# W's third block with its mirrors in one gather, half columns of group two compared on GpSimd, two raw places left early

## The chip, the cores and the metric

The kernel runs on one core of a Trainium2 chip. The metric is the device time of one execution in microseconds (us), the median of three runs. The core's engines are TensorE (PE, matrix products), VectorE (DVE), ScalarE (ACT), GpSimd (POOL) and SyncE (SP). Here SyncE only issues DMA transfers; GpSimd issues gathers (indirect DMAs, which take a row index for each partition) and computes a little.

## The reference

One layer of an FNet block with a routed feed-forward network (FFN), for x of 2048 rows (tokens) by 576 columns, all in float32:

```
a = einsum("bsd,ed->bse", ln(x), dft_hid_re)
b = einsum("bsd,ed->bse", ln(x), dft_hid_im)
h = x + einsum("ts,bse->bte", dft_seq_re, a) - einsum("ts,bse->bte", dft_seq_im, b)
v = ln(h)
r = v @ w_r                               # one score per token
i = argmax(r)                             # capacity 1
y = (silu(v[i] @ w_gate) * (v[i] @ w_up)) @ w_down * sigmoid(r[i])
out = h + v;  out[i] += y
```

The DFT matrices are inputs: 2048 x 2048 and 576 x 576, real and imaginary parts. w_gate and w_up are 576 x 4608, w_down is 4608 x 576; all three are read whole, 31.9 MB.

## The kernel before

**Symmetry, used and tested.** A DFT matrix repeats itself in mirrors: row D - d is row d with the sign of the imaginary part changed, and so are the columns. The kernel computes with a half of each matrix only, and tests on the device, at every run, that the other half is what it should be: it loads the mirrors too, VectorE subtracts (or adds) a block and its mirror into a half of the scratch buffer Q, and ScalarE squares what is left and sums it into a column of DS (`add_square`, L368). If the sum isn't zero, a general path behind a branch at L1358 runs instead.

**The sequence matrix** (dram `ct`) comes in column blocks j = 0 to 15 with a real and an imaginary part i; blocks 1 to 5 form group one, blocks 6, 7, 0 and 8 group two (GROUPS). `c_first` loads a block that is computed with into a place of buffer D (SyncE, L357, 576 KB). `c_check(j, i)` loads its mirrors into raw places, by a gather on GpSimd (L301) and for a pair also by L357 and another gather, and compares: `off_s` (L375) twice and `off_t` (L380). `c_half` compares the halves of a block's own columns with each other: `off_h` (L387), 64 columns of each of 9 row tiles against the other 64. The raw places are the 7 parts of buffer R and those places of D that are free; the function `ring` (L804) hands out the first free one.

**The hidden matrix W** (dram `wt`, 576 rows of 1152: real and imaginary) is loaded by `load_w` in blocks A (rows 0 to 127), B (128 to 255) and C (rows 256 to 288, and the imaginary parts of 256 to 287 once more in partitions 64 to 95); `off_w` (L422 to L427) compares each with its mirror rows, gathered by index column `iw`, and its columns among themselves.

**Computing.** `seq` (L565) multiplies ct's blocks with the normalized, folded x (buffer XF); `keep` (L583) moves the sums into Z; `hid` (L610) multiplies with W; `residual` (L619, VectorE, one operand in PSUM as the name py says) adds x; ScalarE squares for the norm (L630), `dot_h` (L623) forms the scores, `scores` (L635) ends them, and ScalarE and GpSimd write h + v (L661, L654), stored by GpSimd's queue (L676, L678).

**FFN.** The weights come in 27 loads of 1152 KB on SyncE (L1200, and L1208 in two parts) into 17 spots, which are parts of R, D, XF, W, Z and Q that nothing needs any more. For the token VectorE and GpSimd multiply (L1217, L1224; L1228, 14 operations on GpSimd), ScalarE sums (L1233), the gate follows (L1244 to L1247), then TensorE's w_down (L1255) and the last row (L1268, L1278).

**The order.** No order is written by hand: every step is entered in a list (class `Plan`) with its engine, an estimated duration and what it needs, and the list is scheduled. Each engine then runs its instructions in that order, and SyncE and GpSimd each issue their transfers in theirs. An edit of a duration or a need moves steps elsewhere. `turn(n)` is a gather of n rows into a spare tile ahead of a store on GpSimd's queue.

The lines that tie a comparison to its buffers:

```
def ring(eng, f, mb, *args):
    u = free.pop(0)
    ring_last, d = load(eng, then(f, u, *args), mb, users[u], ring_last, LAST[eng])
...
    c_first(1, 1)
    for i in range(2):
        for j in GROUPS[1]:
            c_check(j, i)
    for c, m in HALVES[1]:
        c_half(1, c, m)
```

Of the kernel before, what the change touches and what calls it, by code (L numbers as in the profile page):

```python
# [142 lines left out]
def kernel(  # L143
# [237 lines left out]

    def off_h(g, c, n, i, u):

        o = Q[:, u % 2, i * 9 * n * HM : (i + 1) * 9 * n * HM].rearrange("p (c k m) -> p c k m", k=9, m=HM)
        t = DT[g, i][:, c : c + n]
        for k, op in enumerate((OP.subtract, OP.add)):
            dve.tensor_tensor(o[:, :, k::2, :], t[:, :, k::2, 0:HM], t[:, :, k::2, HM:P], op=op)  # L387

# [8 lines left out]
    def load_w(b, n):  # L397

        name = "ABC"[n % 3]
        if n < 3:  # L400
            t = W[name][:, :, 0:D]
            rows = wt[n * P : n * P + (P if n < 2 else 33), :].rearrange("p (c e) -> p c e", c=2)
            sp.dma_start(t if n < 2 else t[0:33], rows)
            if n == 2:
                sp.dma_start(W[name][64:96, 0, 0:D], wt[2 * P : HD, D : 2 * D])
# [7 lines left out]
    def wrap_w(n):  # L413

        act.activation(W[n][:, :, D : D + 1], W[n][:, :, 0:1], AF.Copy)

    def off_w(n, u):

        ps = W_ROWS[n]
        t, o = WM["ABC"[n]][0:ps], Q[0:ps, u % 2]  # L420
        re, im = W["ABC"[n]][0:ps, 0, :], W["ABC"[n]][0:ps, 1, :]
        dve.tensor_tensor(o[:, 0:D], t[:, 0:D], re[:, 0:D], op=OP.subtract)  # L422
        dve.tensor_tensor(o[:, D : 2 * D], t[:, D : 2 * D], im[:, 0:D], op=OP.add)
        o = o[:, 2 * D : 3 * D]
        dve.tensor_tensor(o[:, 0:287], re[:, 1:HD], re[:, D - 1 : HD : -1], op=OP.subtract)
        dve.tensor_tensor(o[:, 287:575], im[:, 1 : HD + 1], im[:, D - 1 : HD - 1 : -1], op=OP.add)
        dve.tensor_copy(o[:, 575:576], im[:, 0:1])  # L427

    W_ROWS = (P, P, 33)

# [75 lines left out]
    def biases(n0, n1):  # L506

        m, h = n1 - n0, (n1 - n0) // 2
        mean, rs, b = MX[:, n0:n1], RX[:, n0:n1], BX[:, n0:n1]
        pool.tensor_scalar(mean, XT[:, n0:n1], -1.0 / D, None, op0=OP.mult)  # L510
        pool.tensor_tensor(run_of(V0, n0, n1), run_of(MX, n0, n1), x_cols(n0, n1, 0), op=OP.add)
        pool.tensor_scalar(mean, mean, 2.0, None, op0=OP.mult)
        pool.tensor_tensor(b, mean, rs, op=OP.mult)
        q = FOLDED.index(ORDER[n0])
        d0 = XF[:, q : q + (h if n0 < 14 else 2), E0]
# [23 lines left out]
    def folded(k, part):  # L539
# [332 lines left out]

    WS, WL, WRAP = [], [], []

    def w_first():
        for n in range(3):
            LAST["SP"], d = load(
                "SP", then(load_w, None, n), (0.59, 0.59, 0.22)[n], LAST["SP"], users["W" + "ABC"[n]]
            )
            WL.append(d)  # L880

    def w_check():
        for n in range(3):
            u, d = ring("POOL", load_w, (0.59, 0.59, 0.16)[n], n + 3)
# [92 lines left out]
    for c, m in HALVES[0]:  # L977
        c_half(0, c, m)
    for j in GROUPS[0][:3]:
        c_check(j, 0)  # L980
    w_first()
    for j in GROUPS[0][3:]:
        c_check(j, 0)
# [9 lines left out]
    for n in range(3):  # L993
        WRAP.append(add("ACT", 0.25, then(wrap_w, "ABC"[n]), WL[n], SEQ[0, 2][0]))
# [536 lines left out]
```

## Time and profile before

| What | Value |
|---|---|
| median of three runs | 198.0 us (197.77 to 198.25) |
| the profiled execution, its own time | 199.04 us |
| its span, first to last instruction | 197.4 us |
| mean granted TensorE clock | 0.865 of full speed |
| busy: PE, DVE, ACT, POOL | 129.6, 166.6, 140.4, 117.2 us |
| moved by DMA | 77.81 MB, mean 394 GB/s |
| of it hardware queue, software queue (gathers, scattered stores) | 71.5% and 26.5% of the 16 engines' time |

The page cuts the span into 40 equal slices, of 4.9 us each here, and gives for each engine a digit, its busy share in tenths. "DMA" is the same for the mean of the 16 DMA engines, below it what they moved. A window gives the same for a stretch of the span: for each engine busy microseconds and the number of instructions, then the granted clock, the DMA share and GB/s. A row of a timeline has the start, the duration, engine, line and operation, output <- inputs, and in brackets the idle time ahead of it with what ended it. SPq is SyncE's queue: its rows are issues, and the data come later.

### The profile page before, as it was taken

What the parts mean: (1) busy time and instruction counts of PE and PEld (TensorE: products, weight loads), DVE (VectorE), ACT (ScalarE), POOL (GpSimd) and SP (SyncE); (2) the same over time, 40 slices, a digit from 0 to 9 for tenths busy, and PEclk for the clock granted to TensorE, in tenths of its full rate; (3) what the DMA queues carried; (4) which work ended last, traced back from release to release, by engine and by line L of the source; (5) the groups of instructions that cost most, each with busy time, mean ns of one, the idle gap of its engine ahead of it and who ended that gap; (6) DMA issues with size and microseconds to landing.
All of it is one profiled execution on the core that took longest, in us unless ns stands there. A gap on an engine that the chain in (4) does not pass through costs nothing. (4 is left out here: it accounts for less than half of the span.)

```text
span 197.4 us, 2794 instructions
## 1 busy us (share of the span) xinstructions
PE 129.6 (66%) x758; PEld 89.9 (46%) x758; DVE 166.6 (84%) x419; ACT 140.4 (71%) x259; POOL 117.2 (59%) x139
## 2 busy tenths in 40 slices
PE   0007999999999999799999986900232036263940
PEld 0005667754667788477876764700121013031430
DVE  4399996999899968999799999999947999989720
ACT  3198853684699578799389399889555999877630
POOL 6488888284637876359780000003874999999900
PEclk9999999999999999999999999975555555558797
DMA  5999999999899999999999999999999999999992
GB/s 171 408 418 412 413 409 406 411 381 330 281 405 411 411 363 402 400 410 411 416 405 414 418 424 420 426 422 412 424 431 425 420 428 424 422 431 414 412 427 99
DMA packets 14587, 77.81 MB, mean 394 GB/s; under 512 B 1951, under 2 KB 1955, under 8 KB 11239
## 3 DMA queue, kind: packets, MB, share of 16 engines
q1 hardware_dynamic: 10461, 56.56, 71.5%
q0 software_dynamic: 4096, 21.03, 26.5%
q8 instruction: 7, 0.11, 0.2%
q14 instruction: 13, 0.11, 0.1%
q10 hardware_dynamic: 10, 0.00, 0.0%
HBM read 72.86 MB, written 6.49 MB: 402 GB/s over the span
## 5 line engine op out<-in xcount | busy, mean ns | idle before, releaser
L368 ACT ACTIVATE Q<-Q 128x2944 bf16<-128x2944 bf16 (+5 forms) x26 | 55.4, 2132 | 18.5 <-DVE Q L380 8.9
L610 PE MATMUL py<-W,Z 128*128 128x289 f32 x180 | 45.4, 409 | 3.8 <-DVE X L619 3.8
L565 PE MATMUL ps<-D,XF 128*128 128x320 f32 (+3 forms) x216 | 45.0, 408 | 0.5 <-DVE Z L583 0.5
L301 POOL DMA_INDIRECT R<-in_ct_dram,ic x21 | 32.1, 1528 | 17.7 <-DVE Q L375 13.5
L610 PEld LDWEIGHTS py<-W,Z 128*128 128x128 f32 x180 | 33.6, 189 | 15.2 <-issue 4.5
L565 PEld LDWEIGHTS ps<-D,XF 128*128 128x128 f32 (+1 forms) x216 | 32.0, 172 | 13.0 <-issue 1.5
L1228 POOL TENSOR_TENSOR D<-D,Z 128x1152 f32<-128x1152 f32 x8 | 20.9, 2642 | 0.0
L676 POOL DMA_DIRECT2D out_dram<-X x1 | 0.6, 621 | 32.1 <-ACT X L661 32.1
L301 POOL DMA_INDIRECT D<-in_ct_dram,ic x11 | 13.8, 1250 | 7.6 <-DVE Q L380 4.6
L498 ACT ACTIVATE junk<-X,XT 128x576 bf16<-128x576 f32 x16 | 12.3, 771 | 7.8 <-DMA X<-in_x_dram 3.3
L1233 ACT ACTIVATE junk<-D 128x576 bf16<-128x576 f32 x20 | 13.7, 683 | 3.2 <-POOL D L1228 2.6
L1255 PE MATMUL pd<-XF,H 128*1 128x144 f32 x80 | 5.3, 439 | 14.6 <-DVE H L1247 11.3
L537 PE MATMUL fo<-W,diag 128*128 128x288 f32 (+1 forms) x8 | 4.2, 706 | 16.3 <-DVE diag L528 16.3
L375 DVE TENSOR_TENSOR Q<-R,D 128x896 bf16<-128x896 f32 x11 | 11.9, 1084 | 3.2 <-DMA D<-in_ct_dram 1.8
L387 DVE TENSOR_TENSOR Q<-D 128x640 bf16<-128x640 f32 (+3 forms) x20 | 12.8, 691 | 1.7 <-DMA W<-in_wt_dram 1.7
L380 DVE TENSOR_TENSOR Q<-R,D 128x1152 bf16<-128x1152 f32 x10 | 13.4, 1348 | 0.0
L630 ACT ACTIVATE junk<-X,TD 128x576 bf16<-128x576 f32 x16 | 12.3, 766 | 1.4 <-DVE X L619 1.3
L661 ACT ACTIVATE X<-X,BB,UP 128x576 f32<-128x576 f32 x14 | 10.8, 854 | 3.1 <-DVE BB L642 3.1
L623 DVE SCALAR_TENSOR_TENSOR junk<-X,wr 128x576 bf16<-128x576 f32 x16 | 12.1, 755 | 0.3
L375 DVE TENSOR_TENSOR Q<-D 128x896 bf16<-128x896 f32 x11 | 11.8, 1082 | 0.0
L619 DVE SCALAR_TENSOR_TENSOR X<-py,X 128x576 f32<-128x576 f32 x16 | 11.6, 748 | 0.0
L375 DVE TENSOR_TENSOR Q<-R 128x896 bf16<-128x896 f32 x10 | 10.7, 1082 | 0.1
(205 smaller groups left out, 260.8 us busy)
## 6 DMA issues: line engine op xcount, KB each, us to landing
D<-in_ct_dram SPq DMA_DIRECT2D x22, 576.0 KB
R<-in_ct_dram SPq DMA_DIRECT2D x10, 576.0 KB
D<-in_wu_dram SPq DMA_DIRECT2D x5, 1152.0 KB
D<-in_wd_dram SPq DMA_DIRECT2D x4, 1152.0 KB
R<-in_wg_dram SPq DMA_DIRECT2D x3, 1152.0 KB
D<-in_wg_dram SPq DMA_DIRECT2D x3, 1152.0 KB
out_dram<-X SPq DMA_DIRECT2D x2, 1440.0 KB
X<-in_x_dram SPq DMA_DIRECT2D x4, 576.0 KB
```

The lines of the kernel that those rows point to most:

```text
L301: pool.indirect_dma_start(tile, None, view, bass.IndirectOffsetOnAxis(ap=rows, axis=0), element_offset=at)
L368: act.activation(t, t, AF.Square, accum_out=DS[0 : t.shape[0], n : n + 1])
L375: dve.tensor_tensor(o, C[j, i, True][:, 0:7, :], C[j, i, False][:, 7:0:-1, :], op=SIGN[i])
L380: dve.tensor_tensor(o, C[NK - j, i, False], C[j, i, False][:, :, ::-1], op=SIGN[i])
L387: dve.tensor_tensor(o[:, :, k::2, :], t[:, :, k::2, 0:HM], t[:, :, k::2, HM:P], op=op)
L498: act.activation(junk[:, 0:D], X[:, k, 0:D], AF.Square, bias=XT[:, n : n + 1], scale=-float(D), accum_out=VX[:, n : n + 1],)
L565: pe.matmul(cm(ZP[g, n][k % 2][p0 : p0 + m], w), XF[:, q, m0 : m0 + m], DT[g, i][:, :, k, 0:HM], start=k in (0, 1), stop=k in (6, 7),)
L610: pe.matmul(YP[GROUPS[g][c]][:, h, 0:w], Z[:, a, c * P : (c + 1) * P], w_block(a)[:, h * HD : h * HD + w], start=(a == 0), stop=(a == 4),)
L623: dve.scalar_tensor_tensor(junk2, X[:, k, 0:D], 1.0, wr, op0=OP.mult, op1=OP.mult, accum_out=TD[:, n, 0:1])
L630: act.activation(junk[:, 0:D], X[:, k, 0:D], AF.Square, bias=TD[:, n, 1:2], scale=-float(D), accum_out=VAR[:, n : n + 1],)
L1228: pool.tensor_tensor(t, t, xs.unsqueeze(1).to_broadcast([P, JW, D]), op=OP.mult)
L1233: act.activation(junk[:, 0:D], WB[w, j][:, r, :], AF.Copy, accum_out=acc[:, j + r : j + r + 1])
```

## The change

**W's third block.** Blocks A and B start at row 1 (rows 1 to 128, 129 to 256). Block C is rows 257 to 288, and it comes with its mirrors by one gather of 128 half rows (a half row is the real or the imaginary part of a row, 2304 bytes): partitions 0 to 31 rows 257 to 288 real, 32 to 62 their mirrors, 64 to 95 and 96 to 127 the same of the imaginary part. A load of two half rows (the imaginary parts of rows 0 and 288, which must be zero) takes the place of the loads of 33 and 32 rows. `off_wc` compares within the one tile. The columns of XF are laid out anew for the shift by one row, the index column of the gather is made by four iotas, and the fill of W's block C with zeros goes.

**Half columns.** `off_h` of group two runs on GpSimd: eight operations.

**Two raw places.** From the comparison (7, 0) on, places 0 and 1 of the ring are not handed out any more. **The filler** `turn(9)` becomes `turn(4)`.

```
+LEFT = {(7, 0): (0, 1)}
-E0, O0, XF_W = 0, 320, 640
+E1, E_0, O1, XF_W = 0, 319, 320, 640
...
+    wh = wt.rearrange("d (c e) -> (d c) e", c=2)
...
+        pool.memset(iw[:, 2:3], 0)
+        for c in range(2):
+            for p, n, row, step in ((0, 32, D1, 2), (32, 31 + c, D - D1, -2)):
+                pool.iota(iw[64 * c + p : 64 * c + p + n, 2:3], pattern=[[0, 1]], base=2 * row + c, channel_multiplier=step)
...
+    def half_on_pool(g, c, i):
+        return g == 1
     def off_h(g, c, n, i, u):
...
         for k, op in enumerate((OP.subtract, OP.add)):
-            dve.tensor_tensor(o[:, :, k::2, :], t[:, :, k::2, 0:HM], t[:, :, k::2, HM:P], op=op)
+            eng = pool if half_on_pool(g, c, i) else dve
+            eng.tensor_tensor(o[:, :, k::2, :], t[:, :, k::2, 0:HM], t[:, :, k::2, HM:P], op=op)
...
     def load_w(b, n):
-        name = "ABC"[n % 3]
-        if n < 3:
-            t = W[name][:, :, 0:D]
-            rows = wt[n * P : n * P + (P if n < 2 else 33), :].rearrange("p (c e) -> p c e", c=2)
-            sp.dma_start(t if n < 2 else t[0:33], rows)
-            if n == 2:
-                sp.dma_start(W[name][64:96, 0, 0:D], wt[2 * P : HD, D : 2 * D])
-            return
-        t = WM[name] = raw(b, f"w{name}m").rearrange("p a e -> p (a e)")
-        gather(t if n < 5 else t[0:33, :], wt, iw[:, n - 3 : n - 2] if n < 5 else iw[0:33, 2:3])
+        if n < 2:
+            rows = wt[n * P + 1 : (n + 1) * P + 1, :].rearrange("p (c e) -> p c e", c=2)
+            sp.dma_start(W["AB"[n]][:, :, 0:D], rows)
+        elif n == 2:
+            sp.dma_start(W["C"][0:2, 1, 0:D], wh[1 : D + 2 : D, :])
+        elif n < 5:
...
+        else:
+            gather(W["C"][:, 0, 0:D], wh, iw[:, 2:3])
...
+    def off_wc(u):
+        c, o = W["C"][:, 0, :], Q[:, u % 2, 0 : D + 289]
+        dve.memset(o[:, 0:D], 0.0)
+        for p, op in ((0, OP.subtract), (64, OP.add)):
+            dve.tensor_tensor(o[p : p + 31, 0:D], c[p + 32 : p + 63, 0:D], c[p : p + 31, 0:D], op=op)
+        dve.tensor_copy(o[32:34, 0:D], W["C"][0:2, 1, 0:D])
+        off_e(o[:, D:], c[0:64], c[64:P])
...
-        if n == 9:
+        if n == 4:
...
-    dve.memset(W["C"], 0.0)
...
+    shut = set()
     def ring(eng, f, mb, *args):
-        u = free.pop(0)
+        u = [b for b in free if b not in shut][0]
+        free.remove(u)
...
-            add("DVE", 0.16 + 0.62 * m, then(off_h, g, c, m, i, u), [d for _, d in cus[i]], w)
+            add(
+                *(("POOL", 0.3 + 1.31 * m) if half_on_pool(g, c, i) else ("DVE", 0.16 + 0.62 * m)),
+                then(off_h, g, c, m, i, u), [d for _, d in cus[i]], w,
+            )
...
+    def wc_first():
+        LAST["POOL"], d = load("POOL", then(load_w, None, 5), 0.295, LAST["POOL"])
+        WC.append(d)
...
-        for n in range(3):
+        for n in range(2):
...
+    def wc_check():
+        q, w = qs.take()
+        WS.append(add("DVE", 2.6, then(off_wc, q), WL[2], WC, w))
+        squares(q, D + 289, WS[-1])
...
-    for step in "sffsffwsss":
+    for step in "sffsffwcsss":
...
         for j in GROUPS[1]:
+            shut.update(LEFT.get((j, i), ()))
             c_check(j, i)
```

In the listings that follow, each row is a line of the program, an operation, output <- inputs and its shape; the lines of after are shifted by the edits. First SyncE's queue from its sixth transfer on, before; L403 and L405 are the loads of W's blocks (W), L357 loads of ct into raw places (R) and places of D, L1200 the first FFN tiles:

```order
L357 DMA D<-in_ct_dram 128x1152
L403 DMA W<-in_wt_dram 128x2x576 x2
L403 DMA W<-in_wt_dram 33x2x576
L405 DMA W<-in_wt_dram 32x576
L357 DMA D<-in_ct_dram 128x1152
...
L357 DMA R<-in_ct_dram 128x1152 x2
L357 DMA D<-in_ct_dram 128x1152 x5
L357 DMA R<-in_ct_dram 128x1152 x3
L1200 DMA R<-in_wg_dram 128x2304
```

and the same of the changed kernel:

```order
L367 DMA D<-in_ct_dram 128x1152
L415 DMA W<-in_wt_dram 128x2x576 x2
L417 DMA W<-in_wt_dram 2x576
L367 DMA D<-in_ct_dram 128x1152
...
L367 DMA R<-in_ct_dram 128x1152
L367 DMA D<-in_ct_dram 128x1152 x5
L367 DMA R<-in_ct_dram 128x1152 x2
L367 DMA D<-in_ct_dram 128x1152
L367 DMA R<-in_ct_dram 128x1152
L1241 DMA R<-in_wg_dram 128x2304
```

One load of two half rows stands where two loads of 33 and 32 rows stood, and of the last transfers of ct before the first FFN tile one goes to a place of D.

GpSimd's queue of the changed kernel, in two pieces: the gathers of the first checks, and the end of the gathers up to the first store. L311 is a gather (from wt or ct by iw or ic), L401 a half-column comparison, L702 a store:

```order
L311 DMA D<-in_ct_dram,ic 128x896
L311 DMA W<-in_wt_dram,iw 128x576
L311 DMA D<-in_ct_dram,ic 128x896
L311 DMA R<-in_ct_dram,ic 128x896 x7
L311 DMA R<-in_wt_dram,iw 128x1152
L311 DMA D<-in_wt_dram,iw 128x1152
...
L311 DMA spare<-in_x_dram,ix 4x2
L401 TENSOR_TENSOR Q<-D 128x2x5x64
L401 TENSOR_TENSOR Q<-D 128x2x4x64
L702 DMA out_dram<-X 128x1728
```

Before, the first of these pieces had no gather into W and ended in a third gather from wt, of 33 rows into D; and between the filler and the first store GpSimd had nothing. The pair of L401 shown is the last of four.

VectorE of the changed kernel around the comparison of W; L645 is `residual` (before L619), L437 to L446 the comparison of A and B (before L422 to L427), L451 to L454 and the last rows that of C:

```order
L645 SCALAR_TENSOR_TENSOR X,TD<-py_0_535,X 128x576 x2
L437 TENSOR_TENSOR Q<-R,W 128x576
...
L645 SCALAR_TENSOR_TENSOR X,TD<-py_1_556,X 128x576
L451 MEMSET Q 128x288
L453 TENSOR_TENSOR Q<-W 31x576 x2
L454 CAST Q<-W 2x576
L443 TENSOR_TENSOR Q<-W 64x287
L445 TENSOR_TENSOR Q<-W 64x288
L446 CAST Q<-W 64x1
```

Before, the two residuals of py_0 stood between the comparisons of A and B, and C's comparison (five instructions on 33 partitions) followed B's directly, ahead of the residual of py_1.

More of the change, by code (lines that the diff above doesn't have):

```diff
@@ L62 @@
 LATE = 6
-E0, O0, XF_W = 0, 320, 640
+LEFT = {(7, 0): (0, 1)}
+E1, E_0, O1, XF_W = 0, 319, 320, 640
+D1 = 2 * P + 1
 UNIT = 1.0 / D**3
@@ L397, in load_w @@
     def load_w(b, n):
-        name = "ABC"[n % 3]
-        if n < 3:
-            t = W[name][:, :, 0:D]
-            rows = wt[n * P : n * P + (P if n < 2 else 33), :].rearrange("p (c e) -> p c e", c=2)
-            sp.dma_start(t if n < 2 else t[0:33], rows)
-            if n == 2:
-                sp.dma_start(W[name][64:96, 0, 0:D], wt[2 * P : HD, D : 2 * D])
-            return
-        t = WM[name] = raw(b, f"w{name}m").rearrange("p a e -> p (a e)")
-        gather(t if n < 5 else t[0:33, :], wt, iw[:, n - 3 : n - 2] if n < 5 else iw[0:33, 2:3])
+        if n < 2:
[4 more added lines that the diff above has]
+        elif n < 5:
+            name = "AB"[n - 3]
+            t = WM[name] = raw(b, f"w{name}m").rearrange("p a e -> p (a e)")
+            gather(t, wt, iw[:, n - 3 : n - 2])
+        else:
+            gather(W["C"][:, 0, 0:D], wh, iw[:, 2:3])
     def w_block(a):
@@ L413, in wrap_w, with off_e @@
     def wrap_w(n):
-        act.activation(W[n][:, :, D : D + 1], W[n][:, :, 0:1], AF.Copy)
+        c = 1 if n == "C" else 2
+        act.activation(W[n][:, 0:c, D : D + 1], W[n][:, 0:c, 0:1], AF.Copy)
     def off_w(n, u):
-        ps = W_ROWS[n]
-        t, o = WM["ABC"[n]][0:ps], Q[0:ps, u % 2]
-        re, im = W["ABC"[n]][0:ps, 0, :], W["ABC"[n]][0:ps, 1, :]
+        t, o = WM["AB"[n]], Q[:, u % 2]
+        re, im = W["AB"[n]][:, 0, :], W["AB"[n]][:, 1, :]
         dve.tensor_tensor(o[:, 0:D], t[:, 0:D], re[:, 0:D], op=OP.subtract)
         dve.tensor_tensor(o[:, D : 2 * D], t[:, D : 2 * D], im[:, 0:D], op=OP.add)
[L424 to L429, printed above, removed]
+        off_e(o[:, 2 * D : 3 * D], re, im)
+    def off_e(o, re, im):
+        h = o.shape[-1] - 289 if re.shape[0] == P else 0
+        dve.tensor_tensor(o[0 : re.shape[0], 0:287], re[:, 1:HD], re[:, D - 1 : HD : -1], op=OP.subtract)
+        o = o[:, h:] if h else o[64:P]
+        dve.tensor_tensor(o[:, 0:288], im[:, 1 : HD + 1], im[:, D - 1 : HD - 1 : -1], op=OP.add)
+        dve.tensor_copy(o[:, 288:289], im[:, 0:1])
+    def off_wc(u):
[5 more added lines that the diff above has]
+        off_e(o[:, D:], c[0:64], c[64:P])
     VX = mp.tile([P, NK], F32, name="VX")
@@ L514, in biases @@
         q = FOLDED.index(ORDER[n0])
[L515 removed]
+        d0 = XF[:, q : q + (h if n0 < 14 else 2), E_0]
         if n0 == 14:
@@ L696, in then @@
         return lambda: f(*args)
-    dve.memset(XF[:, :, 289 : O0 + 1], 0.0)
-    dve.memset(XF[:, :, O0 + 288 : XF_W], 0.0)
-    dve.memset(W["C"], 0.0)
+    dve.memset(XF[:, :, E1 + 288 : E_0], 0.0)
+    dve.memset(XF[:, :, O1 + 287 : XF_W], 0.0)
     moved = [add("DMA", 1.5, None)]
@@ L871, in c_check @@
         squares(u, QW if j in PAIRS else 7 * P, n)
-    WS, WL, WRAP = [], [], []
+    WS, WL, WRAP, WC = [], [], [], []
     def w_first():
@@ L877, in w_first @@
             LAST["SP"], d = load(
-                "SP", then(load_w, None, n), (0.59, 0.59, 0.22)[n], LAST["SP"], users["W" + "ABC"[n]]
+                "SP", then(load_w, None, n), (0.59, 0.59, 0.005)[n], LAST["SP"], users["W" + "ABC"[n]]
             )
             WL.append(d)
+    def wc_first():
+        LAST["POOL"], d = load("POOL", then(load_w, None, 5), 0.295, LAST["POOL"])
+        WC.append(d)
     def w_check():
-        for n in range(3):
-            u, d = ring("POOL", load_w, (0.59, 0.59, 0.16)[n], n + 3)
+        for n in range(2):
+            u, d = ring("POOL", load_w, 0.59, n + 3)
             q, w = qs.take()
@@ L961, in batch @@
                     continue
-                o = add("POOL", 0.8, then(turn, 9), LAST["POOL"], push=push)
+                o = add("POOL", 0.8, then(turn, 4), LAST["POOL"], push=push)
                 o = add("POOL", 1.3, then(store, k, n, 0, 120), RESULTS, o, push=push)
@@ L978 @@
         c_half(0, c, m)
[L979 to L982, printed above, removed]
+    for n, j in enumerate(GROUPS[0]):
+        if n == 3:
+            w_first()
+        if n == 3:
+            wc_first()
         c_check(j, 0)
@@ L993 @@
     for n in range(3):
-        WRAP.append(add("ACT", 0.25, then(wrap_w, "ABC"[n]), WL[n], SEQ[0, 2][0]))
+        WRAP.append(add("ACT", 0.25, then(wrap_w, "ABC"[n]), WL[n] if n < 2 else WC, SEQ[0, 2][0]))
     no_more("D2")
```

15 lines of the change are left out of this document (7 added, 8 removed).

## The prediction

> **What bounds the kernel now.** I read the profile in this order: the page's forty slices, the windows by stage, the timelines of SyncE, GpSimd and VectorE around the edits, and last the chain of waits. The slices say which resource has no slack:
>
> ```profile
> DVE  4399996999899968999799999999947999989720
> DMA  5999999999899999999999999999999999999992
> GB/s 171 408 418 412 413 409 406 411 381 330 281 405 411 411 363 402 400 410 411 416 405 414 418 424 420 426 422 412 424 431 425 420 428 424 422 431 414 412 427 99
> core 0: us, PE busy (x) PEld busy (x) DVE busy (x) ACT busy (x) POOL busy (x), PEclk, DMA share, GB/s
> 43.00:48.00 5.00, 5.00 (x37) 2.35 (x37) 4.48 (x8) 3.00 (x5) 1.93 (x2) 1.00 1.04 309
> 50.00:54.00 4.00, 4.00 (x16) 2.81 (x16) 3.05 (x5) 2.91 (x3) 2.71 (x2) 1.00 0.83 257
> 55.00:72.00 17.00, 17.00 (x70) 12.72 (x69) 15.09 (x18) 14.13 (x18) 11.92 (x9) 1.00 1.02 411
> 72.00:75.00 3.00, 3.00 (x15) 2.65 (x14) 2.40 (x9) 2.04 (x3) 2.26 (x3) 1.00 1.03 316
> 75.00:105.00 30.00, 28.47 (x140) 22.21 (x140) 28.23 (x45) 23.42 (x31) 19.03 (x14) 1.00 1.02 407
> 105.00:150.00 45.00, 24.48 (x96) 17.15 (x92) 40.52 (x116) 33.82 (x56) 10.09 (x20) 0.78 1.01 422
> 150.00:190.00 40.00, 17.04 (x246) 8.58 (x250) 35.41 (x100) 33.16 (x92) 36.30 (x14) 0.60 1.01 422
> ```
>
> The 16 DMA engines are full from 5 us to the end at 405 to 425 GB/s, apart from three places: 43 to 48 us (309 GB/s), 50 to 54 us (257) and 72 to 75 us (316). In the first and third they are full by time (share 1.04 and 1.03) and yet move less: the transfers themselves are inefficient. In the second they are idle in part (0.83): nothing was queued. So DMA sets the end, and what shortens the kernel is fewer bytes or fewer bad microseconds after 54 us; before 54 us a faster transfer only reaches the second hole sooner.
>
> VectorE is a close second (40.52 of 45 us in 105 to 150), and behind it GpSimd, which from 151 to 187 us multiplies without a pause:
>
> ```profile
> 141.74 0.16 DVE L260 TENSOR_REDUCE gt<-R 128x1 f32<-128x16 f32 x1
> 151.10 2.62 POOL L1228 TENSOR_TENSOR XF<-XF,Z 128x1152 f32<-128x1152 f32 x1 [2.91 <-ACT Z L1103]
> 184.73 2.67 POOL L1228 TENSOR_TENSOR D<-D,Z 128x1152 f32<-128x1152 f32 x1
> 189.58 1.16 PE L1255 MATMUL pd<-D,H 128*1 128x144 f32 x32 [2.08 <-DVE H L1247]
> 192.30 1.12 ACTq L1278 DMA_DIRECT2D out_dram<-orow  x1
> ```
>
> The last scores leave VectorE at 141.74, 9.36 us later GpSimd starts, 36.30 us later (14 operations) it ends, and the row of the FFN goes out at 192.30. This chain of compute and the transfers end within a microsecond or two of each other, so a gain has to come on both.
>
> **The change part by part.** *W's last block.* Two things of before go: the loads of 33 and 32 rows on SyncE, and the mirror gather of 33 rows on GpSimd.
>
> ```profile
> 30.57 2.38 SPq L403 DMA_DIRECT2D W<-in_wt_dram  x3
> 33.88 0.35 SPq L405 DMA_DIRECT2D W<-in_wt_dram  x1
> 64.21 0.94 POOL L301 DMA_INDIRECT D<-in_wt_dram,iw  x1 [0.30 <-issue]
> W<-in_wt_dram SPq DMA_DIRECT2D x1, 148.5 KB
> W<-in_wt_dram SPq DMA_DIRECT2D x1, 72.0 KB
> ```
>
> Issued at 31 to 34 and at 64.2 us, their data pass some ten microseconds later, which is where the first and the third bad stretch lie; I take these three transfers, which fill only 32 or 33 of the 128 partitions, to be their cause. The third: 3 us at 316 GB/s instead of the 409 of its neighbours (411 and 407) lose 3 x (409 - 316) / 409 = 0.68 us. The gather's bytes go too: 33 rows of 4608 bytes are 152 kB, or 0.37 us at 409. Both lie after 54 us, where DMA is dense: **-1.05 us**. The first stretch loses 5 x (410 - 309) / 410 = 1.23 us, but it lies ahead of the second hole, which is closed by VectorE's comparisons; the order of these does not change before 60 us. So I count 0 for it; the other end is the whole 1.23 and a part of the hole's 4 x (410 - 257) / 410 = 1.49. The new gather of 128 half rows (295 kB) is 70 kB more than the two loads' 220.5 KB, 0.17 us at 410, ahead of the same hole: 0, at most +0.17. It takes GpSimd about as long to issue as its neighbours (0.94), which puts off the following gather by 1.25 us with its gap; that gather's data then come into the hole, so at most +1.25 if its comparison had no slack, and I take 0.
>
> [...]
>
> *VectorE.* Half columns of group two, L387, go to GpSimd:
>
> ```profile
> 70.64 0.76 DVE L422 TENSOR_TENSOR Q<-R,W 128x576 bf16<-128x576 f32 x1 [1.82 <-DMA R<-in_wt_dram,iw]
> 72.78 0.75 DVE L619 SCALAR_TENSOR_TENSOR X<-py,X 128x576 f32<-128x576 f32 x1
> ...
> 76.97 0.74 DVE L422 TENSOR_TENSOR Q<-D,W 33x576 bf16<-33x576 f32 x1
> ...
> 79.10 0.74 DVE L619 SCALAR_TENSOR_TENSOR X<-py,X 128x576 f32<-128x576 f32 x1
> 95.14 1.09 DVE L375 TENSOR_TENSOR Q<-R,D 128x896 bf16<-128x896 f32 x1 [1.77 <-DMA D<-in_ct_dram]
> 120.24 1.42 DVE L387 TENSOR_TENSOR Q<-D 128x640 bf16<-128x640 f32 x2
> 122.93 1.42 DVE L387 TENSOR_TENSOR Q<-D 128x640 bf16<-128x640 f32 x2
> 124.94 2.76 DVE L387 TENSOR_TENSOR Q<-D 128x640 bf16<-128x640 f32 x4
> ```
>
> The eight take 1.42 + 1.42 + 2.76 = 5.60 us. The first pair of L619 moves ahead of the first comparison of W and fills 2 x 0.7 = 1.4 us of the 1.82 us wait there. Block C's comparison, 76.97 to 79.10, is 2.1 us; the new one has seven instructions, two of 576 columns (0.7 each), three of 287 to 576 (0.4 each), one of a column (0.1) and a fill of zeros that no row shows, between 0 and a full 0.7: I take 0.3, near the 0.4 of the rows of 288 columns, so 3.0 us, +0.9 (between +0.6 and +1.3). Sum on VectorE: -5.60 - 1.4 + 0.9 = **-6.1 us**, and -7.9 if the 1.77 us wait at 95 goes as well, since DMA is then ahead by 1.05.
>
> *GpSimd.* It gains 5 small operations (some 0.6 us, early, beside rows of 0.2 us) and the eight comparisons:
>
> ```profile
> 28.98 0.27 POOL L513 TENSOR_TENSOR BX<-MX,RX 128x2 f32<-128x2 f32 x1
> 30.63 1.27 POOL L513 TENSOR_TENSOR BX<-MX,RX 128x4 f32<-128x4 f32 x1
> 88.20 4.33 POOL L301 DMA_INDIRECT R<-in_ct_dram,ic  x1 [0.30 <-issue]
> 102.84 1.04 POOL L301 DMA_INDIRECT spare<-in_x_dram,ix  x1 [0.20 <-issue]
> 135.98 0.62 POOL L676 DMA_DIRECT2D out_dram<-X  x1 [32.10 <-ACT X L661]
> ```
>
> They write 4 x 640 + 4 x 512 = 4608 columns; at L1228's 2.64 us for 1152 that is 10.6 us (from below, VectorE's 5.60). GpSimd has nothing to do from 103.9 to 136.0, so even 10.6 us, begun after about 112 when the last full check lets go of its slot, end near 125 and hide. If that cover were gone, each microsecond of delay goes to the stores queued behind them and to the FFN loads that wait for the buffers compared. What no row shows is how the two engines get on when both read pairs of operands from the memory at once. Rows near it: L513 takes 1.27 us, not 0.27, beside back-to-back L387 of VectorE, and the gather 4.33, not about 0.95, beside L375 and L380; VectorE's own rows are not longer there (L387 1.42 for two, as at 120 us). So GpSimd pays, VectorE little. Bounds for VectorE: 0 to +10.6 (it stands still whenever GpSimd reads). I take +4, less than half, because L387 was not slowed and because part of the time VectorE runs L619, which has one operand elsewhere. VectorE's last scores then come 7.9 - 4 = 3.9 us sooner, more than the 1.05 that DMA gains: DMA sets the end.
>
> [...]
>
> *Two raw places left early.* From check (7, 0) on, the ring has five places, and the first FFN tile no longer waits for the last comparisons. Its load is issued now at
>
> ```profile
> 101.46 0.33 SPq L1200 DMA_DIRECT2D R<-in_wg_dram  x1
> ```
>
> and DMA around it is full (407 GB/s to 105, 422 behind), because GpSimd's gathers fill it. A load that comes sooner only changes places with others: 0. Between -0.3 (were there a gap of one issue) and +1.77 (five places instead of seven starve a comparison as the row at 95.14 shows); I take 0, as the neighbours are full.
>
> **Sum.** The profiled execution takes 199.04 us, a span of 197.4 and 1.6 around it, and lies 1.04 above the median 198.0. 199.04 - 1.05 = 198.0, a span of 196.3; on the median, 198.0 - 1.05 = **196.9 us**.
>
> **The rivals.**
>
> *The early holes come back too (B).* If the comparisons at 50 to 54 us wait for data of the slow loads rather than for VectorE's order, 1.23 and part of 1.49 are gained: 1.05 + 1.23 + 0.3 = 2.6, or 195.4. For it: GpSimd and SyncE both feed that stretch. Against it: share 0.83, the queue was empty, which faster data before it cannot cure.
>
> *Only bytes (C).* The change does not do what it says: the bad stretch at 72 to 75 has another cause (the first two W mirrors pass nearby too) and stays, or VectorE loses all that it saved. Then 0.37 us or less is left, 197.7; for it speaks that windows don't tell transfers apart.
>
> *GpSimd and VectorE stand still for each other (D), slower.* Place: the comparisons at 112 to 130 us. VectorE pays 10.6 against the 7.9 it saves: +2.7, its last scores come at 144.4 and the unbroken 9.36 + 36.30 us behind them shift with it: 198.0 + 2.7 = 200.7; with half the loss on VectorE and GpSimd starved so that the stores behind its comparisons and the loads into their buffers open a DMA hole of a microsecond, about 198.8. It decides from a loss of VectorE above 7.9 us, or when the comparisons end after about 130. For it: 1.27 and 4.33 show contention. Against it: VectorE's rows did not stretch.
>
> **How the numbers follow.** Forecast 196.9 with its own 196.3 to 197.5: 0.45. B, 195.4: 0.15. C, 197.7: 0.18. D, 198.6 to 200.7: 0.22. Two in ten may be left out: 195.3 to 199.8 takes in B and the nearer half of D. About 0.2% (0.4 us) is what a measurement of this kernel can tell from no change, so faster is below 197.6: forecast and B, 0.60; within: C, 0.18; slower, above 198.4: D, 0.22.
>
> **What would show it.** In the changed profile the windows at 72 to 75 should have 400 GB/s or more, with the stretch at 43 to 48 recovered and the hole behind it as wide or wider; VectorE's last scores should come near 138 and GpSimd's first product near 147; L375, L380 and L623 between 112 and 130 should last what they last now, and GpSimd's comparisons about 1.2 to 1.5 us each. I am wrong if the third stretch stays, if the rows of VectorE grow beside those comparisons, or if DMA has a new hole between 95 and 135 us.

## The result, and the profile after

The changed kernel is slower: 201.12 us, median of six runs (199.49 to 202.13), against 198.24 for the kernel before in the same comparison. The ratio is 1.0121, 95% interval 1.0086 to 1.0156. A second comparison on another chip gave 200.28 against 199.51, 1.0055 (1.0011 to 1.0099). The profiled execution took 199.49 us with a span of 197.8 and was the fastest of its six, so its span hides a part of the loss. A second profile of the same kernel (200.48 us, span 198.8) stands below where it differs. A ratio leaves out the executions that took over 1.5% more than the fastest of their kernel, so it need not be the quotient of the medians beside it.

Windows of the changed kernel (busy microseconds and instructions of each engine, granted clock, DMA share, GB/s):

```profile
core 0: us, PE busy (x) PEld busy (x) DVE busy (x) ACT busy (x) POOL busy (x), PEclk, DMA share, GB/s
43.00:48.00 5.00, 5.00 (x38) 2.54 (x35) 5.00 (x7) 1.46 (x4) 1.55 (x1) 1.00 1.00 396
50.00:54.00 4.00, 4.00 (x16) 2.81 (x16) 3.05 (x5) 4.00 (x3) 1.53 (x3) 1.00 0.92 312
72.00:75.00 3.00, 3.00 (x16) 2.64 (x15) 2.96 (x8) 2.69 (x5) 2.24 (x2) 1.00 1.02 408
0.00:95.00 95.00, 78.22 (x321) 57.14 (x322) 81.43 (x191) 66.44 (x106) 59.12 (x103) 1.00 1.00 394
142.00:190.00 48.00, 20.95 (x238) 10.43 (x238) 40.16 (x123) 38.26 (x98) 42.15 (x28) 0.52 0.99 403
155.00:160.00 5.00, 1.07 (x20) 0.69 (x24) 4.79 (x15) 4.78 (x14) 5.00 (x3) 0.50 0.88 305
160.00:165.00 5.00, 1.02 (x21) 0.30 (x10) 4.86 (x14) 4.75 (x14) 5.00 (x3) 0.50 1.00 354
```

and two windows of the kernel before:

```profile
0.00:95.00 95.00, 76.38 (x310) 55.07 (x311) 80.47 (x189) 66.90 (x106) 63.67 (x98) 1.00 0.99 382
142.00:190.00 48.00, 20.53 (x254) 10.68 (x258) 39.72 (x121) 37.12 (x98) 41.35 (x27) 0.59 1.01 423
```

The two bad stretches are gone (309 became 396 GB/s, 316 became 408). By 95 us the DMA engines have moved 95 x (394 - 382) = 1140 kB more, a lead of 2.8 us at 410 GB/s. But the one profile of before is a poor yardstick for this. Its hole at 50 to 54 us (257 GB/s) is missing in the profiles of e4, e6 and e13 below, which load W as before does (404 to 406 GB/s), and these have 388 to 390 GB/s up to 95 us. Two windows of e13, then one of the second profile of the changed kernel:

```profile
50.00:54.00 4.00, 4.00 (x17) 2.81 (x16) 3.04 (x5) 4.00 (x3) 1.53 (x3) 1.00 1.02 404
0.00:95.00 95.00, 77.88 (x317) 56.47 (x318) 81.79 (x191) 67.03 (x106) 63.12 (x100) 1.00 1.00 390
0.00:95.00 95.00, 75.09 (x300) 54.31 (x301) 81.42 (x191) 66.09 (x105) 63.47 (x103) 0.98 0.99 385
```

Against 389 the lead is 95 x (394 - 389) / 410 = 1.2 us in the first profile of the changed kernel, and in the second there is none (385). What made the hole in the profile of before is not known.

Between 142 and 190 us the engines move 48 x (423 - 403) = 960 kB less than in the profile of before: a hole at 155 to 165 us that was not there swallows 2.0 us. The loads at 156 us and after wait for places that the products free, and so for compute: here DMA was ahead and compute was not, and the lead ended in the hole (305 and 354 GB/s). Two other profiles agree. In e1 the first product comes as late (152.52 us), but DMA lost its lead at 95 to 105 us, and there is no hole; in e12, which kept the lead, there is one (334 and 367 GB/s). Two windows of e1:

```profile
95.00:105.00 10.00, 7.53 (x27) 5.76 (x25) 8.96 (x14) 5.59 (x5) 5.90 (x6) 0.83 0.89 342
155.00:160.00 5.00, 0.93 (x19) 0.56 (x22) 4.79 (x15) 4.78 (x14) 5.00 (x3) 0.50 1.00 412
```

Why compute came late is seen in VectorE's timeline of the changed kernel (first profile), from the last full checks to the last scores (L385 is before's L375, L649 its L623, L258 to L260 its L248 to L250, L665 its L639):

```profile
94.17 1.09 DVE L385 TENSOR_TENSOR Q<-D,R 128x896 bf16<-128x896 f32 x1 [3.21 <-DMA R<-in_ct_dram]
...
120.04 1.98 DVE L649 SCALAR_TENSOR_TENSOR junk<-X,wr 128x576 bf16<-128x576 f32 x1
122.06 1.70 DVE L649 SCALAR_TENSOR_TENSOR junk<-X,wr 128x576 bf16<-128x576 f32 x1
...
126.27 1.28 DVE L258 SCALAR_TENSOR_TENSOR uh<-VAR,r0h 128x6 f32<-128x6 f32 x1
127.58 1.19 DVE L259 SCALAR_TENSOR_TENSOR uh<-uh,r0h 128x6 f32<-128x6 f32 x1
128.81 1.46 DVE L260 SCALAR_TENSOR_TENSOR RS<-uh,r0h 128x6 f32<-128x6 f32 x1
130.18 1.30 DVE L665 SCALAR_TENSOR_TENSOR R<-TD,wsum 128x6 f32<-128x6 f32 x1
...
142.41 0.18 DVE L270 TENSOR_REDUCE gt<-R 128x1 f32<-128x16 f32 x1
```

The rows of 6 columns take 0.17 to 0.22 us where nothing runs beside them, those of L649 0.75. Here six rows last 6.7 us longer than that (1.23 + 0.95 + 1.11 + 1.02 + 1.29 + 1.08). They stand beside GpSimd's comparisons. The timeline of GpSimd and SyncE in the same kernel (start, duration, engine, line, operation, in brackets the idle time ahead and what ended it):

```profile
115.30 7.86 POOL L401 TENSOR_TENSOR Q<-D 128x640 bf16<-128x640 f32 x4 [11.01 <-ACT Q L378]
125.93 5.53 POOL L401 TENSOR_TENSOR Q<-D 128x640 bf16<-128x640 f32 x4 [2.78 <-ACT Q L378]
143.47 0.33 SPq L1241 DMA_DIRECT2D Q<-in_wg_dram  x1
152.38 2.62 POOL L1269 TENSOR_TENSOR XF<-XF,Z 128x1152 f32<-128x1152 f32 x1 [2.97 <-ACT Z L1144]
156.34 0.35 SPq L1241 DMA_DIRECT2D R<-in_wu_dram  x1
```

Both sides pay: the second four, undisturbed by anything long, take 5.53 us; the first four, with checks of VectorE between them, 7.86. The last scores come at 142.41 (before 141.74), GpSimd's first product at 152.38 (151.10). The load into Q, which needs ScalarE's squares of the last half columns, is issued at 143.47; it was 133.50. The second profile repeats the comparisons to within a hundredth (7.86 and 5.52; 1.98, 1.70, 1.27, 1.19, 1.45, 1.30 on VectorE).

L649 and the small rows have two inputs in SBUF and are stretched; L645 with its one operand in PSUM is not (four rows of 0.74 to 0.75 us from 116.06 us on, beside GpSimd's first four). Who pays differs from row to row: L390 at 117.41 us has two inputs in SBUF as well and lasts its usual 1.36 us, and GpSimd's first four, beside it, are the ones that last longer (7.86 us for 5.53).

### The profile page after: what moved, and what is told of

Read it like the earlier page. It is cut to its first block, busy times and chain, and to the rows that moved or that the text cites. A ratio compares the mean times of both kernels' runs of the same rounds, so it can differ in the third digit from the quotient of the medians.

```text
span 197.8 us, 2791 instructions
## 1 busy us (share of the span) xinstructions
PE 131.6 (67%) x758; PEld 91.2 (46%) x758; DVE 168.7 (85%) x412; ACT 140.3 (71%) x259; POOL 125.1 (63%) x151
## 5 line engine op out<-in xcount | busy, mean ns | idle before, releaser
L591 PE MATMUL ps<-D,XF 128*128 128x320 f32 (+3 forms) x216 | 46.7, 417 | 1.9 <-DVE Z L609 1.9
L591 PEld LDWEIGHTS ps<-D,XF 128*128 128x128 f32 (+1 forms) x216 | 33.3, 178 | 14.8 <-DVE Z L609 2.3
L311 POOL DMA_INDIRECT R<-in_ct_dram,ic x21 | 24.1, 1148 | 17.1 <-DVE Q L385 13.2
L311 POOL DMA_INDIRECT D<-in_ct_dram,ic x11 | 15.5, 1409 | 12.9 <-DVE Q L385 5.7
L401 POOL TENSOR_TENSOR Q<-D 128x640 bf16<-128x640 f32 (+1 forms) x8 | 13.4, 1703 | 13.8 <-ACT Q L378 13.8
L1269 POOL TENSOR_TENSOR D<-D,Z 128x1152 f32<-128x1152 f32 x7 | 18.2, 2632 | 0.0
L385 DVE TENSOR_TENSOR Q<-R,D 128x896 bf16<-128x896 f32 x14 | 15.1, 1086 | 1.4 <-ACT Q L378 1.4
L649 DVE SCALAR_TENSOR_TENSOR junk<-X,wr 128x576 bf16<-128x576 f32 x16 | 14.3, 891 | 0.3
L1274 ACT ACTIVATE junk<-D 128x576 bf16<-128x576 f32 x16 | 10.9, 683 | 2.8 <-POOL D L1269 2.3
L390 DVE TENSOR_TENSOR Q<-R,D 128x1152 bf16<-128x1152 f32 x9 | 12.1, 1352 | 0.0
L645 DVE SCALAR_TENSOR_TENSOR X<-py,X 128x576 f32<-128x576 f32 x16 | 11.6, 750 | 0.0
L1258 DVE SCALAR_TENSOR_TENSOR junk<-R,xsp 128x576 bf16<-128x576 f32 x14 | 10.5, 752 | 0.3
L1296 PE MATMUL pd<-D,H 128*1 128x144 f32 x128 | 7.5, 400 | 4.9 <-DVE H L1288 4.9
```

The source lines that it names most:

```text
L311: pool.indirect_dma_start(tile, None, view, bass.IndirectOffsetOnAxis(ap=rows, axis=0), element_offset=at)
L385: dve.tensor_tensor(o, C[j, i, True][:, 0:7, :], C[j, i, False][:, 7:0:-1, :], op=SIGN[i])
L401: eng.tensor_tensor(o[:, :, k::2, :], t[:, :, k::2, 0:HM], t[:, :, k::2, HM:P], op=op)
L591: pe.matmul(cm(ZP[g, n][k % 2][p0 : p0 + m], w), XF[:, q, m0 : m0 + m], DT[g, i][:, :, k, 0:HM], start=k in (0, 1), stop=k in (6, 7),)
L649: dve.scalar_tensor_tensor(junk2, X[:, k, 0:D], 1.0, wr, op0=OP.mult, op1=OP.mult, accum_out=TD[:, n, 0:1])
L1269: pool.tensor_tensor(t, t, xs.unsqueeze(1).to_broadcast([P, JW, D]), op=OP.mult)
```

## The experiments

Ratios are to the kernel before on the same chip, with their 95% intervals; e1 to e4, e5 to e8, e9 to e11 and e12 to e13 shared a chip each.

| Run | What | Median us | Ratio |
|---|---|---|---|
| after | the change | 201.12 | 1.0121 (1.0086 to 1.0156) |
| e1 | after, half columns on VectorE | 199.02 | 1.0002 (0.9969 to 1.0035) |
| e2 | after, seven raw places to the end | 201.28 | 1.0156 (1.0110 to 1.0202) |
| e3 | before with W's loads alone | 200.96 | 1.0133 (1.0093 to 1.0174) |
| e4 | before with half columns on GpSimd alone | 199.49 | 1.0038 (1.0014 to 1.0061) |
| e5 | after, half columns of group two left out | 199.37 | 1.0025 (0.9984 to 1.0066) |
| e6 | before with the two raw places alone | 198.18 | 0.9981 (0.9946 to 1.0016) |
| e7 | after, comparisons cut into 36 pieces | 200.28 | 1.0067 (1.0030 to 1.0105) |
| e8 | after, fills instead of comparisons | 198.11 | 0.9945 (0.9910 to 0.9980) |
| e9 | e1, four loads behind one full check | 200.92 | none, see there |
| e10 | e1, four loads behind two full checks | 209.58 | 1.0490 (1.0412 to 1.0568) |
| e11 | after again | 200.28 | 1.0055 (1.0011 to 1.0099) |
| e12 | after, only the first four on GpSimd | 198.71 | 1.0023 (0.9992 to 1.0054) |
| e13 | e6 with the first four on GpSimd | 198.36 | 1.0028 (0.9993 to 1.0063) |

### e1 to e4 and e6: the three parts apart

```
e1     def half_on_pool(g, c, i):
-          return g == 1
+          return False
e2 -   LEFT = {(7, 0): (0, 1)}
   +   LEFT = {}
e3     both, and turn(9) again
e4 (on the kernel before)
-      dve.tensor_tensor(o[:, :, k::2, :], ...)
+      (pool if g == 1 else dve).tensor_tensor(o[:, :, k::2, :], ...)
...
e6 (on the kernel before; ring as in the change)
...
+              shut.update(LEFT.get((j, i), ()))
               c_check(j, i)
```

> The changed kernel with group two's half columns back on VectorE; the gather of W's last block and the two raw places stay. Theory 1, contention (six VectorE rows between 120 and 132 us stretched by 6.7 us in all, and the load into Q 11.6 us late behind GpSimd's last comparison): VectorE pays 5.6 us again but loses no 6.7, the last scores come about 1 us sooner than in the changed kernel, no row of 18 columns lasts over 0.3 us, and the time is at or below before, 197 to 198. Theory 2, the two raw places (VectorE waits 3.2 us for a load at 94 us): the time stays near the changed kernel's 201.

> The changed kernel with all seven raw places handed out to the end; half columns still on GpSimd. Theory 2, raw places: the wait of 3.2 us at 94 us shrinks to 1.8 us or less and the time falls to about 199. Theory 1, contention: the stretched rows stay, 200 to 201.

> Only the new loads and comparison of W's last block; half columns on VectorE, seven raw places, the filler of nine rows. As predicted for this part: the stretch at 72 to 75 us at 400 GB/s or more, 196.9 (1.05 us less than before). If the new gather or its comparison is what costs: above 199.

> The kernel before with nothing changed but the half columns of group two on GpSimd. Theory 1, contention alone makes the loss: 200 to 201, with rows of VectorE stretched by 5 to 8 us in all while the eight comparisons run. If contention needs the other parts, or if it is theory 2: 198 or less, since VectorE saves 5.6 us.

> The kernel before with nothing changed but the two raw places left early. By the prediction 0: 198 to 199. If they are what made e1 1.3% faster than e3, without W's new loads too: 196 to 197.

The times speak for theory 1: e1 is level with before, which after is not by either of its comparisons (though e1's interval and that of e11 overlap). Its eight comparisons take 2.76 us for four, and no small row is stretched. But the profile of e1 does not show the gain that was expected. Its last scores come at 143.27, not a microsecond sooner than after's 142.41 and 143.33, since VectorE waits 4.30 us at the check near 96 us where after's first profile has 3.21. So no trace here shows which microseconds e1's median of 199.02 saves (the profiled execution took 199.83).

Theory 2 has its part: e1 and e3 differ in the two raw places (and in the filler, of four rows in e1 and nine in e3), and by 1.3%. Inside the change the same two places are worth less: e2 lies 0.3% above after and 1.0% above e11, and its interval overlaps the first. The wait near 95 us did not shrink in e2 as theory 2 had it, it grew to 4.86 us; the stretched rows stayed, and the last scores came at 145.21. And W's loads alone, e3, which the prediction put at 0.5% faster, are 1.3% slower. Timeline of e3: GpSimd's gather of W's second mirror, VectorE's wait for it, SyncE's first FFN tile:

```profile
61.39 6.64 POOL L311 DMA_INDIRECT D<-in_wt_dram,iw  x1 [0.30 <-issue]
75.03 0.76 DVE L437 TENSOR_TENSOR Q<-D,W 128x576 bf16<-128x576 f32 x1 [4.28 <-issue]
105.64 0.33 SPq L1241 DMA_DIRECT2D XF<-in_wg_dram  x1
```

and two windows of e3, columns as before:

```profile
85.00:90.00 5.00, 2.36 (x11) 1.55 (x10) 5.00 (x9) 4.32 (x6) 2.77 (x2) 1.00 0.92 319
105.00:110.00 5.00, 5.00 (x36) 3.40 (x33) 4.53 (x10) 3.91 (x10) 0.00 (x0) 1.00 0.91 321
```

Two things happened that no term of the prediction had. First, with W's new loads and seven places the ring turns out otherwise than before, and the first FFN tile no longer goes to R but to XF, which TensorE still reads (in e3 SyncE's FFN loads wait up to 10.3 us for L591): it is issued at 105.64 instead of 101.46, and DMA loses 5 x (410 - 321) / 410 = 1.1 us there. In e2, with seven places too, it is the same (XF, 309 GB/s from 105 to 110 us). In e1, e6 and after the tile goes to R. So the two raw places are worth nothing by themselves (e6, 0.9981 with 1 inside the interval, as predicted) and mend a hole that W's new loads open. Second, the wait ahead of W's first comparison (1.82 us before) is filled, and the gather issued at 61 us meets a VectorE that runs comparisons without a pause. It takes 6.64 us here and in the second profile of the changed kernel, and 1.09 in the first profile, with the same instructions on VectorE. The new loads are not its condition: e6, with W's loads as before, has such a gather too (5.58 us at 61 us). The gather in the timeline of the first profile:

```profile
61.07 1.09 POOL L311 DMA_INDIRECT D<-in_wt_dram,iw  x1 [0.30 <-issue]
```

and of the second (e11), with VectorE's wait for it:

```profile
61.15 6.64 POOL L311 DMA_INDIRECT D<-in_wt_dram,iw  x1 [0.30 <-issue]
74.23 0.76 DVE L437 TENSOR_TENSOR Q<-D,W 128x576 bf16<-128x576 f32 x1 [3.73 <-issue]
```

In each profile with the new loads VectorE waits some 2.3 to 4.9 us, either there or at the check near 95 us (3.21 in after's first profile). In before, e4 and e13, which have the old loads, two waits, one ahead of W's first comparison and one near 95 us, add up to 3.6 to 4.6 us. So the wait that the residuals fill comes back in another place. The last scores of e3 come at 142.85. How much of e3's 1.3% is the hole at 105 us and how much the wait was not taken apart.

e4 says that the half columns alone cost 0.4%, inside the change 1.2% or 0.5% (e1 against after, or against e11) and 0.2% without the two raw places (e3 against e2), all with wide intervals; the expectation of 200 to 201 was too high. In e4's profile seven rows of VectorE between 121 and 131 us are stretched by 7.0 us (0.95 + 1.22 + 0.16 + 1.30 + 1.02 + 1.35 + 1.02), much as in after, for the 5.6 it saves.

### e5, e7 and e8: what stretches VectorE's rows

```
e5 -   for c, m in HALVES[1]:
   -       c_half(1, c, m)
e7 +   for k in range(9):
   +       pool.tensor_tensor(o[:, :, k, :], t[:, :, k, 0:HM], t[:, :, k, HM:P], op=...)
e8 -   eng.tensor_tensor(o[:, :, k::2, :], ...)
   +   pool.memset(o[:, :, k::2, :], 0.0)
```

> The changed kernel without the comparison of group two's half columns: neither engine does it (its eight operations and two squares are left out). Theory 1, contention, with VectorE's last scores as what sets the end: against e1 VectorE has 5.6 us less to do and no contention, so the last scores come near 137 to 138 us, and the time falls until the transfers set the end: 195 to 196.5. If DMA sets the end already: no change against e1, 198.5 to 199.

> The changed kernel with each comparison on GpSimd cut into pieces of one row tile: 36 operations of 128 columns for eight of 512 or 640. Theory 1a, VectorE's instruction waits until the one of GpSimd that runs has ended: the small rows of 6 columns (1.2 to 1.5 us beside the comparisons) fall to 0.3 to 0.5 us, and the time to about 198 to 199. [...]

> The changed kernel with a fill of zeros in place of each of the eight comparisons on GpSimd (the half columns of group two are not compared): it writes the same places and reads nothing. If it is GpSimd's reading that stands against VectorE's second operand: VectorE's rows in the same stretch at their usual length (0.17 and 0.75 us), last scores some 5 us sooner, 196 to 198. If writing contends as well: rows stay stretched, 200 to 201.

e8 shows that it is GpSimd's reading that stretches VectorE's rows. GpSimd writes the same places, VectorE's rows beside it are at their plain length (0.76 and 0.17 us below), and the last scores come 4 us sooner (138.34 for 142.41). The timeline of e8, GpSimd, then VectorE:

```profile
115.06 2.12 POOL L401 MEMSET Q<- 128x640 bf16 x4 [10.91 <-ACT Q L378]
123.98 2.14 POOL L401 MEMSET Q<- 128x640 bf16 x4 [6.80 <-ACT Q L378]
124.27 0.76 DVE L647 SCALAR_TENSOR_TENSOR X<-py,X 128x576 f32<-128x576 f32 x1 [1.81 <-PE py L638]
124.95 0.76 DVE L651 SCALAR_TENSOR_TENSOR junk<-X,wr 128x576 bf16<-128x576 f32 x1
125.85 0.17 DVE L258 SCALAR_TENSOR_TENSOR uh<-VAR,r0h 128x6 f32<-128x6 f32 x1
138.34 0.19 DVE L270 TENSOR_REDUCE gt<-R 128x1 f32<-128x16 f32 x1
```

The fills are shorter than the comparisons (2.1 us for 5.5), so fewer of VectorE's rows stand beside them; but the rows at 124.95 and 125.85, with two SBUF inputs each (L651 is before's L623, L258 its L248), run beside the second four and last 0.76 and 0.17 us. Freed of the contention, VectorE runs into a new wait, for TensorE (1.81 us at 124 us and 0.77 at 129). The time, 0.55% below before, is what the prediction gave to the change. The end is another one too. TensorE's last wait in the timeline of after, then of e8:

```profile
190.84 1.16 PE L1296 MATMUL pd<-W,H 128*1 128x144 f32 x32 [1.36 <-DVE H L1288]
189.91 0.67 PE L1298 MATMUL pd<-W,H 128*1 128x144 f32 x16 [0.62 <-DMA W<-in_wd_dram]
```

In after it waits for the gate, as in before (L1247), so compute sets the end; in e8 it waits for the last weights, so the transfers do. How much of the 0.55% is the contention is not shown, since e5, which leaves out the fills as well, is not faster.

e7 speaks for theory 1a: with pieces of 128 columns, 21.80 / 36 = 0.61 us each, the small rows from 127.05 us on take 0.38 to 0.50 us, instead of the 1.2 to 1.5 beside comparisons of 5.53 / 4 = 1.38 us. A shorter instruction of GpSimd made VectorE wait less, as it would if VectorE waits until that instruction has ended. The time did not fall to the 198 to 199 that were expected: the ratio lies between the two of the changed kernel, and the last scores at 142.78 are no sooner. The 36 pieces last until 137.9 us, so many more of VectorE's rows stand beside them. The timeline of e7:

```profile
116.06 21.80 POOL L402 TENSOR_TENSOR Q<-D 128x128 bf16<-128x128 f32 x36 [10.94 <-ACT Q L378]
127.05 0.38 DVE L259 SCALAR_TENSOR_TENSOR uh<-uh,r0h 128x6 f32<-128x6 f32 x1
127.77 0.49 DVE L669 SCALAR_TENSOR_TENSOR R<-TD,wsum 128x6 f32<-128x6 f32 x1
142.78 0.16 DVE L270 TENSOR_REDUCE gt<-R 128x1 f32<-128x16 f32 x1
```

One of e7's twelve executions took 745.95 us, of which there is no profile; it stays unexplained.

e5 missed. The last scores came at 135.95, even sooner than expected, but the time did not fall. VectorE's last row in the timeline of e5 waits for TensorE:

```profile
192.00 0.37 DVE L1307 SCALAR_TENSOR_TENSOR orow<-pd,sg,orow 97x144 f32<-97x144 f32 x1 [4.70 <-PE pd L1294]
```

In after this wait is 1.91 us. With the scores 6 us early something behind them sets the end, most likely the last weights as in e8 (argued, not shown), and leaving out work of VectorE buys nothing any more. The FFN tiles go to other spots in e5, so its transfers are not those of e1.

### e9 and e10: the wait near 95 us

```
-  no_more("D0")
-  c_first(1, 1)
   for i in range(2):
       for n, j in enumerate(GROUPS[1]):
+          if (i, n) == (0, 1):          # e10: (0, 2)
+              no_more("D0")
+              c_first(1, 1)
```

> As e1 (the changed kernel, half columns on VectorE), but the four loads of group two's imaginary blocks stand behind the loads of the first full check of group two instead of ahead of them. Theory 3, what W's faster loads gain is lost in front of that check: VectorE arrives 2 us sooner and waits 3 to 4 us for a mirror that is queued behind those four loads. Then the wait near 94 to 96 us falls below 1.5 us, the last scores come 2 us or more sooner than e1's 143.3, and the time is 197 or less. If the wait only moves to the next check: as e1, 198 to 199.

> As e9, but the four loads stand behind two full checks. Theory 3: as e9 or a little better in VectorE's waits. If TensorE needs these blocks by then: a new wait of TensorE near 95 to 105 us, and the time above e1's.

Theory 3 was not confirmed. In e9's profile the wait at 95 us is gone, but VectorE waits 4.86 us at 76 us behind a gather of 6.64 us, as in e3, and the last scores come at 144.61. One of its six executions took 196.93 us and five 200.54 to 201.82, too far apart for a ratio; the profiled one (201.38) is of the five, so the waits of the short one are not known. e10 shows what the four loads are for, in TensorE's timeline:

```profile
104.90 1.62 PE L591 MATMUL ps<-D,XF 128*128 128x256 f32 x3 [6.85 <-DMA D<-in_ct_dram]
```

The rival of its expectation came true: 4.9% slower. Why VectorE waits near 95 us although DMA is ahead stays open.

### e11: after again

> The changed kernel once more, beside these two on the same chip, for a second profile (its first was the fastest of its six executions) and a narrower ratio: 1.2% slower than before, VectorE's rows between 115 and 135 us stretched by 6 to 7 us again, the load into Q issued after 140 us.

The stretched rows and the late load (144.39) came again. The ratio of 1.0055 is smaller than the first; the two intervals overlap between 1.0086 and 1.0099.

### e12 and e13: is there a better placement?

```
e12    def half_on_pool(g, c, i):
-          return g == 1
+          return g == 1 and c == 0
e13    the same on e6
```

> The changed kernel with the first four of the eight comparisons on GpSimd and the second four on VectorE. If contention's price lies in what runs beside: the four small rows at 126 to 132 us are back at 0.2 us (4.4 us less), VectorE pays 2.8 us for the four comparisons, and the last scores come 1.5 us sooner than in the changed kernel's same execution (142.4 or 143.3): 199 to 200, between e1 and the changed kernel or at e1. If any use of GpSimd here costs the same: as the changed kernel, 200 to 201.

> The kernel before with the two raw places left early and the first four comparisons on GpSimd; W's loads as before. From e6 (198.2) VectorE saves 2.8 us and loses about 2.2: the last scores at 140.5, and the time within 0.3% of e6.

With the second four back on VectorE the small rows are at 0.17 to 0.22 us again, and e12 is level with before, a little below the 199 to 200 that were expected. The last scores come at 141.89, 0.5 us sooner than in after's first profile, whose gather and wait are alike, and not 1.5. But now the two engines compare half columns at the same time; the timeline of e12, GpSimd and VectorE:

```profile
117.53 6.64 POOL L401 TENSOR_TENSOR Q<-D 128x640 bf16<-128x640 f32 x4 [13.43 <-ACT Q L378]
119.17 6.29 DVE L401 TENSOR_TENSOR Q<-D 128x640 bf16<-128x640 f32 x4
```

and for comparison VectorE's four in e1, where GpSimd does none:

```profile
121.90 2.76 DVE L401 TENSOR_TENSOR Q<-D 128x640 bf16<-128x640 f32 x4
```

VectorE's four take 6.29 instead of 2.76 us: 3.5 lost for 2.8 saved. e13 lies 0.5% above e6 by their ratios, with intervals that overlap; its last scores come at 141.26, as e6's do (141.14), and not at the 140.5 that were expected. No version here beats the kernel before by more than its interval, save e8, which leaves the comparison out.

## Why the prediction was wrong

- **W's bytes and the two bad stretches**: right that they went with W's old loads. With the new loads alone (e3) there are 415 GB/s at 70 to 75 us, where e4 and e6 have 375 and 361. That the old ones pass badly because they fill only 32 or 33 partitions was my estimate; no run takes this apart. At 40 to 50 us the four profiles with the old loads have 354 to 360 GB/s, the two of the changed kernel 401 and 402. The size of 1.05 us is near the 1.2 us by which the first profile is ahead at 95 us of those of e4, e6 and e13; 2.8 us, against the profile of before alone, counts that profile's own hole. The second profile is not ahead at all. Counting 0 for the first stretch was about right: the changed kernel still has a hole behind it (312 and 315 GB/s), where e4, e6 and e13 have none (404 to 406).
- **"-1.05 us, since DMA is dense after 54 us"** failed. Dense is not the same as bounding: the transfers here wait for places that VectorE and, in the FFN, the products free. The lead was given back at 155 to 165 us in after (305 and 354 GB/s), at 105 and 85 us in e3 (321 and 319), at 95 to 105 us in e1 (342). "DMA sets the end" holds in few profiles: TensorE's last wait names a transfer in e8, and in e2 (0.30 us).
- **VectorE: "I take +4 ... because L387 was not slowed"** is the step that made it slower instead of level, as far as the times of e1 and e12 against after show it, and e4, which is slower with this part alone. VectorE lost 6.7 us in two profiles. That a row with one operand elsewhere is spared was assumed there; L645, at 0.74 to 0.75 us beside GpSimd's first four, bears it out. The rows that showed VectorE unharmed (L387, L375 beside a slow GpSimd) show, as I read them now, only the case in which GpSimd came second and waited (L513 began at 30.63 us, the L387 beside it at 30.43; for the gather, begun at 88.20 us with L375 at 88.35, this is not shown); short rows beside a GpSimd comparison of 1.4 us did not exist in the profile of before.
- **"fills 1.4 us of the 1.82 us wait" and "-7.9 if the 1.77 us wait goes"**: the first wait was filled, but the second grew to 3.21, or turned up as 3.73 in front of W's second comparison. With -5.6 + 6.7 on top, the last scores came 0.67 us later (1.59 in the second profile), not 3.9 sooner, so compute set the end. Why the wait comes back stays open.
- **Two raw places, 0**: right alone (e6), wrong beside W's new loads, where they save 1.3% (e3 against e1), or 0.3 to 1.0% with the half columns on GpSimd (e2).
- **Rival D** named what happened (VectorE lost 6.7 us, GpSimd's first four took 7.86 for 5.53) and the place; its price (10.6 us for VectorE) was too high, and the point from which it decides (7.9) too high as well, for it was reckoned with the wait that did not go. That its 200.7 came near what was measured is in part luck: a smaller loss of VectorE, and a smaller gain. e8 (0.55% below before, which makes 196.9 of 198.0) shows that the forecast's time was in reach where GpSimd doesn't read, though e8 doesn't do the comparison, and e5, without it too, did not reach that time.

## What to carry to other kernels

Where two engines hold each other up, an absence of harm in the trace is read only from the side that came second: look for short instructions of the one that will stand behind long ones of the other, and count a whole instruction of wait for each (here 1.02 to 1.29 us for each small row, beside comparisons of 5.53 / 4 = 1.38 us). A transfer queue that is full all along may still be paced by the buffers that compute frees, so a gain in bytes counts only as far as the compute behind it moves too (here 394 GB/s up to 95 us, then 305 at 155 to 160 us). And a change of how many places are in use turns the whole rotation: look at which buffer the next phase's first load falls into (here XF with 321 GB/s in e3, R with no such hole in after). Last, a hole seen in one profile of the kernel before may be that execution's own: a second profile, or one of a variant that is alike up to there, tells (here 257 GB/s, against 404 to 406 in e4, e6 and e13).

## What the runs showed of the hardware that was not expected

- The same gather with the same instructions around it took 1.09 us in one profile and 6.64 in another of the same kernel; the long ones end about when VectorE leaves its run of two-operand comparisons (from 60.3 to 66.9 us in the second profile; the gather ends at 67.8). That the comparisons hold it up is argued from the place, not shown.
- When both engines compared from SBUF at once (e12), VectorE took 6.29 us for 2.76 and GpSimd 6.64 for 5.5: together, from 117.53 to 125.46 us, they needed about as long as one after the other (5.5 + 2.76).
- GpSimd's writing alone cost VectorE nothing that can be seen (e8: 0.76 and 0.17 us beside the fills).
